# A new instruction order for a retention and WaveMLP kernel: 34 DMA transposes in place of 39, and products of zeros moved ahead

## The chip, the cores and the metric

The kernel runs on one core of one Trainium2 chip. The metric is the device time of one execution in microseconds (us), lower is better; the median over several runs is compared. The core has five engines with instruction queues of their own: TensorE (PE in the profile; its weight loads are PEld), VectorE (DVE), ScalarE (ACT), GpSimd (POOL) and SyncE (SP), which here only issues DMAs. Each queue runs strictly in its own order and waits for others by semaphores.

## The reference

Inputs are q, k, v of shape (4, 8, 768, 64) in float32 (batch, heads, tokens, head width) and four weight matrices. First a linear attention with a decay for each head, then a mixing layer over tokens and channels:

```python
gamma = 1.0 - 2.0 ** (-5.0 - np.arange(H))
for t in range(S):
    state = gamma * state + einsum('bhd,bhe->bhde', k[:, :, t], v[:, :, t])
    y[:, :, t] = einsum('bhd,bhde->bhe', q[:, :, t], state) / np.sqrt(D)
x = y.transpose(0, 2, 1, 3).reshape(B, S, H * D)      # (4, 768, 512)

theta = x @ w_theta
zr, zi = x * cos(theta), x * sin(theta)
u = x + w_tok_r @ zr + w_tok_i @ zi                   # over tokens, in each batch
out = u + maximum(u @ w_ch, 0)
```

The output is (4, 768, 512) in float32.

## The kernel before

The whole program is a list of small functions, and one string, ORDER, says in which order they are called. Since the tile framework is used with its scheduler switched off, a token's place in ORDER is its place in the queues of the engines that it uses: two tokens on the same engine run in the order of the string, two on different engines are tied only by the data and buffers that they share. A token such as `cq.3.p` calls `cq(3, "p")`; the last letter names the engine (p POOL, v DVE, a ACT, s SP).

**Attention.** The work is cut into 24 units: batch, then three blocks of 256 tokens, then two halves of four heads. Unit n is loaded by `Lk`, `Lq` and `Lv` (256 KB each, L156, all on SP's queue), cast or scaled to bf16 by `ck`, `cq` and `cv` (L138, L278, L284), and its k and q are transposed: either on TensorE (`Tk` and `Tq`, four transposes each into one PSUM tile, then one copy `E`), or by one DMA transpose (`Dk`, L308) that SP issues. `G(n)` puts three groups of sixteen small products together: the scores of unit n (at, L322), the output inside the block of unit n-1 (L392) and the state's increment of unit n (L350). `m` masks the scores on DVE (L331), `SU` adds to the state (L362 to L366), `SB` casts the state to a block diagonal bf16 tile sbd (L138 on DVE or POOL, L136 on ACT), `I` multiplies the queries with it (L379), and `XA` copies the result out of PSUM to xT, x transposed (L412).

**Mixing.** For each of 24 blocks C of 128 tokens, `Tx` and `Ex` (TensorE and a copy) or `Dx` (a DMA transpose, L433) turn xT into x; `Hh` makes theta (four products of 512 columns, L440), `CN` takes the sine and cosine on ACT (L447), and `z` multiplies both with x (L454, DVE or POOL). `M(t, s0)` is two products of 512 columns into the output block t for the token block s0 (L487), so block t needs the six z of its batch. `u` adds x (L494), `Tu` and `Eu` or `Du` (a DMA transpose, L509) transpose u, `O` multiplies by w_ch (four products, L514), `f` takes the maximum and adds (L520), and `SO` stores 256 KB from SP's or ACT's queue (L525). The last block is cut into two halves (`Mh`, `uh`, `Tuh`, `Euh`, `Oh`, `fh`, `SOh`), and ends the program.

**Weights.** `Lth` and `Lch` load w_theta and w_ch (1 MB each, `cth` and `cch` cast them in quarters), `Lw` loads 128 rows of w_tok_r or w_tok_i, `cw` casts, `Tw` transposes on TensorE and `Ew` copies out of PSUM.

**Constants and zero products.** `const2` makes the exponents' input (POOL, then one multiplication on DVE), `const3` the two scale tables by two exponentials on ACT, which cq and cv need; `const4` the identity, `const5` the mask, `const1` a tile of zeros and `const6` zeros in sbd. `warm(n)` multiplies the tile of zeros with itself n times into a PSUM tile that nobody reads:

```python
    def warm(n):
        t = psum.tile([P, dm], FT, name="y_ps", tag="y", bufs=1)
        for _ in range(n):
            nc.tensor.matmul(t, K["zero"][:, :P], K["zero"], start=True, stop=True)
```

Buffers tie tokens as well. All transposes through PSUM, and theta of the odd blocks from 7 on, share two PSUM buffers (tag tr), so each waits until the one two before it was copied out; y uses one bank and o another (acc) for most of the program, so `M.t.0` waits for `u` of the block before. kf, qf and vf have nine buffers each, kqT four, uT three.

## Time and profile before

| what | value |
|---|---|
| median of 5 runs | 175.66 us |
| lowest and highest | 174.13 and 177.23 us |
| the profiled execution's own time | 174.13 us |
| its span, first to last instruction | 172.2 us |
| mean granted TensorE clock | 0.970 |
| TensorE, DVE, ACT, POOL busy | 153.1, 116.1, 80.2, 83.3 us |
| DMA transposes: kqT, x_sb, uT | 10, 12, 17 |

The span is 1.9 us shorter than the execution's time; what lies around it doesn't depend on the order. The profile page has the busy time of each engine; slices of the span in which a digit is the busy share in tenths (PEclk is the clock granted to TensorE, in tenths of full speed); the chain of waits, followed back from the last instruction; and groups of instructions with the mean of one in ns and what ended the idle time before them. Matmuls overlap, so the length of one product (379 ns for 512 columns) is more than the 216 ns from one start to the next.

### The profile page before, as it was taken

How to read it: one execution, taken by the hardware profiler on the slowest of the kernel's cores; microseconds unless marked ns; L12 is line 12 of the kernel's file. 1: busy time of each engine (PE TensorE's matmuls, PEld its weight loads, DVE VectorE, ACT ScalarE, POOL GpSimd, SP SyncE). 2: the span in 40 equal slices, each digit the busy share in tenths (PEclk: the TensorE clock that was granted, in tenths of full speed). 3: DMA queues.
4: the chain of work that ended last, by engine and by line, in shares of the span. 5: the costliest groups of instructions: out<-in, count | busy, mean ns of one | idle time of the engine just before them, and what ended most of it. 6: DMA issues, size and time to landing. Idle time of an engine off the chain costs nothing.

```text
span 172.2 us, 4849 instructions
## 1 busy us (share of the span) xinstructions
PE 153.1 (89%) x1996; PEld 87.4 (51%) x1996; DVE 116.1 (67%) x191; ACT 80.2 (47%) x157; POOL 83.3 (48%) x106
## 2 busy tenths in 40 slices
...
PEclk9995769999999999999999999999999999999999
...
GB/s 139 279 290 291 352 328 286 335 365 263 201 245 350 330 207 207 250 289 293 162 274 181 232 163 216 153 317 183 227 177 122 182 108 142 73 232 30 183 162 173
DMA packets 70757, 38.71 MB, mean 225 GB/s; under 512 B 28112, under 2 KB 65232, under 8 KB 70736
## 3 DMA queue, kind: packets, MB, share of 16 engines
...
## 4 chain that ended last, share of the span: by engine, by line
PE 69%; DVE 9%; DMA 8%; SPq 7%; issue 2%; POOLq 1%; ACT 1%; DVEq 0%; ACTq 0%
PE y_ps L487 29%; PE o_ps L514 11%; PE th_ps L440 11%; SPq L156 7%; DMA w<-in_moe_w_theta_dram 5%; PE at_ps L322 4%; DMA x_sb<-xT 3%; PE r_ps L392 3%; DVE sbd L138 2%; PE r_ps L379 2%; PE kq_ps L292 2%; PE y_ps L537 2%; PE r_ps L350 1%; DVE z L454 1%; DVE at L331 1%
## 5 line engine op out<-in xcount | busy, mean ns | idle before, releaser
L487 PE MATMUL y_ps<-z,wtr 128*128 128x512 bf16 x138 | 52.4, 380 | 1.6 <-POOL z L454 1.4
L487 PE MATMUL y_ps<-z,wti 128*128 128x512 bf16 x138 | 52.3, 379 | 0.0
L278 POOL TENSOR_TENSOR kqb<-qf,qsc 128x512 bf16<-128x512 f32 x21 | 22.9, 1091 | 17.6 <-DMA qf<-in_q_dram 17.5
L331 DVE TENSOR_TENSOR at<-at_ps,mask 128x1024 bf16<-128x1024 f32 x24 | 29.2, 1216 | 1.2 <-PE at_ps L322 1.1
L412 ACT CAST xT<-r_ps 128x256 bf16<-128x256 f32 x48 | 17.1, 374 | 27.3 <-PE r_ps L350 15.7
L440 PE MATMUL th_ps<-wth,xT 128*128 128x512 bf16 x96 | 25.4, 397 | 1.2 <-ACT wth L136 1.2
L520 DVE SCALAR_TENSOR_TENSOR ot<-o_ps,u 128x512 f32<-128x512 f32 x23 | 15.8, 687 | 11.8 <-PE o_ps L514 11.3
L494 DVE TENSOR_TENSOR u<-y_ps,x_sb 128x512 bf16<-128x512 f32 x23 | 15.7, 687 | 11.8 <-PE y_ps L487 11.6
L514 PE MATMUL o_ps<-wch,uT 128*128 128x512 bf16 x92 | 23.5, 380 | 0.0
L454 POOL TENSOR_TENSOR z<-cs,x_sb 128x1024 bf16<-128x1024 bf16 x7 | 15.3, 2186 | 15.0 <-DMA x_sb<-xT 8.7
L487 PEld LDWEIGHTS <-wti 128*128 128x128 bf16 x138 | 13.5, 98 | 14.7 <-issue 2.5
L447 ACT ACTIVATE cs<-th_ps,zerob 128x512 bf16<-128x512 f32 x24 | 16.4, 689 | 9.1 <-PE th_ps L440 6.8
L138 POOL CAST kqb<-kf 128x512 bf16<-128x512 f32 x19 | 14.3, 757 | 12.4 <-DMA kf<-in_k_dram 11.7
L487 PEld LDWEIGHTS <-wtr 128*128 128x128 bf16 x138 | 13.5, 98 | 13.0
L284 POOL TENSOR_TENSOR vb<-vf,vsc 128x512 bf16<-128x512 f32 x16 | 17.8, 1120 | 3.5 <-PE y_ps L487 3.0
L447 ACT ACTIVATE cs<-th_ps,halfpi 128x512 bf16<-128x512 f32 x24 | 16.5, 689 | 5.2 <-PE th_ps L440 2.6
L454 DVE TENSOR_TENSOR z<-cs,x_sb 128x1024 bf16<-128x1024 bf16 x17 | 15.3, 907 | 1.5 <-ACT cs L447 1.4
L292 PE MATMUL kq_ps<-ident,kqb 128*128 128x128 bf16 x112 | 11.3, 245 | 5.0 <-DVE kqb L138 4.3
L440 PEld LDWEIGHTS <-xT 128*128 128x128 bf16 x96 | 9.3, 101 | 11.0 <-issue 3.0
L514 PEld LDWEIGHTS <-uT 128*128 128x128 bf16 x92 | 8.5, 98 | 9.7 <-DMA uT<-u 0.3
L322 PE MATMUL at_ps<-kqT 64*64 64x128 bf16 x384 | 10.5, 229 | 3.0 <-ACT kqT L136 1.9
L292 PEld LDWEIGHTS <-kqb 128*128 128x128 bf16 x112 | 8.4, 109 | 8.2 <-DVE kqb L138 4.3
...
## 6 DMA issues: line engine op xcount, KB each, us to landing
...
```

The source lines that it names most:

```text
L138: engines[e].tensor_copy(dst, src)
L278: engines[e].tensor_mul(in_blocks(kqb_of(n)[:, 1]), by_token(raw["qf", n]), _bcast_last(K["qsc"][:, i, :, h * HU:(h + 1) * HU], D))
L284: engines[e].tensor_mul(in_blocks(vb), by_token(raw["vf", n]), _bcast_last(K["vsc"][:, i, :, h * HU:(h + 1) * HU], D))
L292: nc.tensor.transpose(st["kq_ps", n][:, 4 * w + x, :], st["kqb", n][:, w, x * P:(x + 1) * P], K["ident"])
L322: nc.tensor.matmul(at_ps[cols, g, j, a, :], kqT[rows, 0, a, j, cols], kqT[rows, 1, :, j, cols], start=(j == 0 and a == 0), stop=(j == 1 an ...
L331: nc.vector.tensor_mul(at.rearrange("p g j a t -> p (g j) (a t)"), st["at_ps", n].rearrange("p g j a t -> p (g j) (a t)"), _bcast_mid(K["m ...
L412: nc.scalar.copy(st["xT", 2 * i + c][:, 2 * h:2 * h + 2].rearrange("p j (t a) -> p j t a", a=2), st["R", n + 1][:, c, :2 * P].rearrange("p ...
L440: nc.tensor.matmul(th_ps, st["xT", C][:, j, :], K["wth"][:, j, :], start=(j == 0), stop=(j == 3))
L447: nc.scalar.activation(st["cs", C][:, w, :], st["th_ps", C], AF.Sin, bias=K["zerob" if w else "halfpi"], scale=1.0)
L454: engines[e].tensor_mul(st["z", b][:, c], st["cs", C], _bcast_mid(x_of(C), 2))
L487: nc.tensor.matmul(st["y", t], K["wT"][r][:, s0, t0 * P:(t0 + 1) * P], st["z", b][:, s0, r, :], start=(s0 == 0 and r == 0), stop=(s0 == nT ...
L514: nc.tensor.matmul(o_ps, st["uT", t][:, j, :], K["wch"][:, j, :], start=(j == 0), stop=(j == nD - 1))
```

## The change

Only the string ORDER differs. No function is changed, and every needed token is there once; what a token does may be on another engine. Counted from the two strings:

| tokens | before | after |
|---|---|---|
| zero products (calls of warm) | 8 (1) | 44 (8) |
| Dk, Dx, Du | 10, 12, 17 | 11, 9, 14 |
| Tk and Tq, Tx, Tu | 14 and 14, 12, 6 | 13 and 13, 15, 9 |
| SB on ACT, DVE, POOL | 23, 14, 11 | 25, 19, 4 |
| z on DVE, POOL | 17, 7 | 20, 4 |
| cv on DVE, POOL | 8, 16 | 3, 21 |
| Ew on DVE, ACT | 8, 4 | 11, 1 |
| Ex on DVE, ACT | 8, 4 | 6, 9 |
| Eu on DVE, ACT | 3, 3 | 3, 6 |
| SO on SP, ACT | 11, 12 | 14, 9 |

The first eight zero products come ahead of all other work of TensorE, where before the transposes of the first k were ahead of them; the other 36 stand in seven groups up to the first theta products. `const2` moves behind `const4`, `ck.0` and `const5` on POOL. The diff, cut:

```diff
--- before.py
+++ after.py
 ORDER = """
-const2 Lk.0.s const1 Lq.0.s Lv.0.s const3 const6 const4 ck.0.v cv.0.v const5 Tk.0 Lk.1.s Lq.1.s
-cq.1.p warm.8 Lv.1.s Lk.2.s Lq.2.s cq.0.v Lv.2.s cv.1.v Tq.0 ck.1.a E.0.a cq.2.p Lk.3.s G.0 SU.0
-ck.3.p SB.0.0.v ck.2.a Tk.1 Lq.3.s cv.2.p cq.3.p SB.0.1.a Tq.1 I.0 m.0 E.1.a G.1 Tk.2 Lv.3.s
-Lk.4.s Lq.4.s Tq.2 Tk.3 XA.0.1 SU.1 E.2.v m.1 ck.4.v cq.4.p SB.1.0.a SB.1.1.a Lv.4.s XA.0.0 Tq.3
-I.1 G.2 SU.2 SB.2.1.a Lth.s m.2 SB.2.0.p Lw.0.0.s cv.3.p Lk.5.s XA.1.1 XA.1.0 Lq.5.s E.3.v cth.2.a
-Tq.4 cv.4.p Lv.5.s Tk.4 cth.1.p Lw.1.0.s cw.0.0.p ck.5.p cth.0.a I.2 Lk.6.s G.3 Lq.6.s XA.2.1
-cth.3.v cq.5.p Lw.0.1.s m.3 SU.3 Tx.0 Hh.1 E.4.a Lv.6.s cv.5.p SB.3.0.v cw.1.0.p Hh.0 Tx.1 Ex.0.a
-XA.2.0 SB.3.1.v I.3 Lk.7.s G.4 Ex.1.v ck.6.p Tq.5 CN.0.1 CN.0.0 XA.3.1 Tk.5 m.4 E.5.a cq.6.p SU.4
-Lq.7.s Tw.0.0 cw.0.1.p cv.6.p SB.4.1.a SB.4.0.v Tw.1.0 Ew.0.0.v XA.3.0 CN.1.1 Ew.1.0.v Tk.6 I.4
-z.0.v ck.7.p G.5 Tq.6 SU.5 SB.5.1.p cq.7.p CN.1.0 Lw.1.1.s Lv.7.s E.6.v m.5 Lk.8.s Hh.3 SB.5.0.a
-Tx.3 Hh.2 XA.4.0 Tx.2 Ex.3.v CN.3.1 Lq.8.s z.1.p Ex.2.v Lw.0.2.s Lw.1.2.s XA.4.1 Lw.0.3.s ck.8.p
-CN.3.0 I.5 G.6 Tq.7 cw.1.1.a cq.8.p XA.5.1 Tk.7 E.7.a Tw.1.1 Tx.5 XA.5.0 CN.2.1 m.6 CN.2.0 Lv.8.s
-z.3.v Ew.1.1.v SU.6 cw.0.2.p Hh.5 Tx.4 Ex.5.v cv.7.v Lw.1.3.s SB.6.0.a Tk.8 Lk.9.s Lq.9.s Hh.4
-Ex.4.v SB.6.1.a CN.5.0 CN.5.1 Tq.8 z.2.v Lv.9.s I.6 G.7 Tw.0.2 M.0.0 Lk.10.s CN.4.1 CN.4.0 Lq.10.s
-E.8.v z.5.p Lw.0.4.s Tw.0.1 M.0.1 cw.1.2.p cv.8.p SU.7 ck.9.p M.0.2 cq.9.p M.0.3 SB.7.1.v cw.0.3.a
-XA.6.1 Ew.0.2.v z.4.v SB.7.0.v Lv.10.s Tw.0.3 XA.6.0 m.7 Ew.0.1.a M.0.4 ck.10.p Ew.0.3.a M.0.5 u.0
...
-Lch.s M.1.2 M.1.3 SB.8.1.v Tu.0 Lq.11.s Ew.1.3.a M.1.4 XA.7.1 cv.9.p M.1.5 ck.11.p cch.0.p Lv.11.s
...
-CN.6.1 Ex.7.a CN.6.0 M.3.0 Tk.11 cch.1.a m.10 Du.1 SU.10 M.3.1 M.3.2 Ew.0.4.v SB.10.0.v M.3.3
-Lq.13.s Lv.13.s Tq.11 XA.9.1 E.11.v XA.9.0 ck.12.p M.3.4 M.3.5 z.7.p ck.13.p Tx.6 cw.1.4.a
-SB.10.1.a Tw.1.4 I.10 cch.2.a u.3 G.11 Ew.1.4.a O.0 Ex.6.v XA.10.0 Lk.14.s cq.13.p SU.11 Tw.0.5
-Lq.14.s M.4.0 Ew.0.5.v Tx.9 M.4.1 Dx.8 m.11 XA.10.1 M.4.2 M.4.3 Lv.14.s Lk.15.s Dk.13 Tq.12 M.4.4
-SB.11.1.a Ex.9.a Tk.12 cw.1.5.a Hh.9 cv.12.v E.12.a M.4.5 SB.11.0.v Lq.15.s f.0 Lv.15.s CN.9.0
-I.11 CN.9.1 Tw.1.5 G.12 u.4 O.1 XA.11.0 Ew.1.5.v M.5.0 SU.12 M.5.1 z.6.p Tu.2 XA.11.1 f.1 cq.14.p
...
-m.23 M.13.3 Dx.20 XA.22.0 M.13.4 SO.11.s CN.21.0 O.16 CN.21.1 SO.9.s Dx.21 SB.23.1.p SB.23.0.p
-I.23 G.24 M.13.5 XA.23.1 f.16 XA.23.0 Dx.22 O.12 M.22.0 f.12 Du.15 z.20.v u.13 Dx.23 Hh.23 z.21.p
-Hh.22 CN.23.0 M.20.0 M.22.1 CN.22.0 M.18.0 M.20.1 M.18.1 M.18.2 CN.22.1 CN.23.1 M.22.2 M.18.3
-M.22.3 O.14 z.22.v SO.10.s M.18.4 M.22.4 z.23.p M.20.2 M.22.5 M.18.5 Du.13 f.14 u.18 u.22 O.15
-M.20.3 SO.16.a Du.18 SO.14.a M.17.0 M.17.1 M.19.0 f.15 SO.12.s M.19.1 O.13 Du.22 M.17.2 M.17.3
-f.13 M.17.4 M.17.5 M.19.2 SO.13.a u.17 M.20.4 M.19.3 O.18 f.18 M.21.0 M.19.4 M.19.5 M.21.1 O.22
-M.21.2 u.19 M.21.3 SO.15.s M.21.4 M.21.5 Du.17 f.22 O.17 Du.19 u.21 M.20.5 f.17 u.20 O.19 Mh.0.0
-Mh.1.0 Mh.0.1 f.19 SO.22.a Mh.0.2 Mh.0.3 SO.18.a Mh.0.4 Du.21 Du.20 Mh.1.1 Mh.1.2 Mh.1.3 Mh.0.5
-uh.0 SO.19.a Mh.1.4 Mh.1.5 O.21 O.20 Tuh.0 uh.1 SO.17.a f.21 SO.21.s Tuh.1 Euh.0 f.20 Euh.1 Oh.0
-SO.20.a Oh.1 fh.0 fh.1 SOh.1 SOh.0
+const4 Lk.0.s ck.0.p const1 const5 Lq.0.s Lv.0.s const6 const2 Lk.1.s const3 warm.8 cq.0.v cv.0.p
+Tk.0 Lq.1.s ck.1.p Lv.1.s Lk.2.s cv.1.p Lq.2.s cq.1.v warm.6 Tq.0 E.0.a warm.5 Tk.1 G.0 cq.2.p
+Tq.1 ck.2.v SU.0 E.1.a Lw.0.0.s SB.0.0.a Lv.2.s Lk.3.s ck.3.p warm.9 Tq.2 Lq.3.s cq.3.p SB.0.1.a
+m.0 Lv.3.s I.0 cv.2.v Lk.4.s G.1 Lq.4.s SU.1 SB.1.1.p ck.4.p Lth.s Tk.2 m.1 XA.0.0 XA.0.1 Lw.1.0.s
+warm.9 Tq.3 E.2.v cv.3.v Tk.3 SB.1.0.a cq.4.p E.3.a I.1 G.2 SU.2 XA.1.0 Lv.4.s SB.2.1.p SB.2.0.p
+Lk.5.s cth.0.p Lq.5.s cth.3.p cw.1.0.p cv.4.p Tk.4 XA.1.1 warm.3 Tx.0 m.2 Tq.4 E.4.v Lv.5.s warm.1
+I.2 cw.0.0.a cth.2.v Ex.0.a cth.1.a G.3 SU.3 Lw.0.1.s Lk.6.s ck.5.p XA.2.1 cq.5.p cv.5.p Lq.6.s
+Tw.0.0 Lv.6.s Lw.1.1.s XA.2.0 SB.3.1.a cw.0.1.p warm.3 Hh.0 Tw.1.0 Lk.7.s SB.3.0.v CN.0.0 m.3
+CN.0.1 Ew.1.0.v Lq.7.s Hh.1 cq.6.p Ew.0.0.v I.3 G.4 Tk.5 Lv.7.s Lk.8.s Tq.5 CN.1.1 z.0.v Lw.0.2.s
+SU.4 CN.1.0 XA.3.1 E.5.a m.4 Tx.1 Hh.3 cv.6.p Ex.1.v SB.4.1.v Lq.8.s SB.4.0.a Lw.1.2.s XA.3.0
+Lw.0.3.s Tw.0.1 ck.6.a Tx.3 CN.3.1 z.1.v CN.3.0 I.4 Ex.3.v G.5 Lv.8.s Ew.0.1.v SU.5 Hh.2 m.5
+cw.1.1.p ck.7.p XA.4.0 cq.7.p Tq.6 Tk.6 Lw.1.3.s cv.7.p ck.8.p cw.0.2.p SB.5.0.v cq.8.p Lk.9.s
+XA.4.1 SB.5.1.a Lq.9.s Tx.2 E.6.v Lv.9.s I.5 z.3.v Ex.2.a G.6 CN.2.0 Tw.1.1 Tq.7 Lw.0.4.s CN.2.1
+Tk.7 Lch.s XA.5.1 Lk.10.s m.6 XA.5.0 Hh.5 Ew.1.1.v Lq.10.s SU.6 E.7.a SB.6.0.a Tx.5 cw.1.2.p
+CN.5.1 CN.5.0 SB.6.1.v Hh.4 I.6 Tw.0.2 Ex.5.v z.2.v CN.4.1 z.5.p CN.4.0 Lw.1.4.s cv.8.p Ew.0.2.v
+G.7 cq.9.p Lv.10.s Tx.4 SU.7 M.0.0 ck.9.p cv.9.p Ex.4.v cch.2.p cw.0.3.v Tk.8 z.4.v Tq.8 Lk.11.s
+M.0.1 Lq.11.s ck.10.p XA.6.0 E.8.a SB.7.1.v SB.7.0.a cq.10.p M.0.2 XA.6.1 cq.11.p m.7 Tw.0.3
+Lv.11.s M.0.3 M.0.4 M.0.5 u.0 Tw.1.2 Lw.0.5.s I.7 cw.1.3.v G.8 M.1.0 M.1.1 M.1.2 M.1.3 SU.8
+Ew.1.2.v M.1.4 Ew.0.3.a Lk.12.s Tu.0 XA.7.0 Tq.9 m.8 M.1.5 SB.8.1.v Eu.0.v Hh.6 Tk.9 SB.8.0.v
+cw.0.4.a Tw.1.3 Lq.12.s u.1 XA.7.1 ck.11.p M.2.0 CN.6.0 E.9.v M.2.1 I.8 Ew.1.3.v ck.12.p cch.1.a
+cq.12.p G.9 cv.11.p cch.3.v cch.0.v Lw.1.5.s Dk.11 CN.6.1 Lv.12.s SU.9 M.2.2 Hh.7 cw.1.5.p m.9
+CN.7.1 Tx.6 Ex.6.v M.2.3 M.2.4 SB.9.0.v SB.9.1.v M.2.5 cv.12.p Dk.12 u.2 O.0 XA.8.0 Lk.13.s CN.7.0
+f.0 Tk.10 M.3.0 XA.8.1 Tq.10 I.9 ck.13.p Tw.0.4 Lq.13.s cw.1.4.v E.10.a cv.10.v M.3.1 M.3.2 M.3.3
+Tw.1.4 Ew.0.4.v G.10 Lv.13.s Tu.1 Eu.1.a Lk.14.s M.3.4 Ew.1.4.v M.3.5 m.10 Tx.7 u.3 XA.9.1 O.1
+XA.9.0 Tx.8 M.4.0 SU.10 M.4.1 SB.10.0.a Ex.7.v M.4.2 Ex.8.a Lq.14.s cq.13.p ck.14.p SB.10.1.v
+M.4.3 cw.0.5.a Lv.14.s Tu.2 M.4.4 Dk.13 Eu.2.a cv.13.p z.7.v Tw.0.5 f.1 cq.14.p I.10 Tx.9 G.11
+Ex.9.a z.6.v cv.14.p Hh.8 Ew.0.5.v Tw.1.5 SU.11 m.11 M.4.5 Hh.9 XA.10.0 SB.11.1.a Ew.1.5.v XA.10.1
+SB.11.0.a I.11 CN.8.1 u.4 G.12 CN.9.0 XA.11.1 M.5.0 Lk.15.s Lq.15.s CN.8.0 CN.9.1 SU.12 Lv.15.s
+M.5.1 Dk.14 Tx.11 Lk.16.s M.5.2 cq.15.p M.5.3 Ex.11.a Lq.16.s z.8.v z.9.v Tu.3 O.2 SB.12.1.v f.2
+Eu.3.a cq.16.p SB.12.0.a M.5.4 XA.11.0 SO.0.a Lv.16.s M.5.5 Hh.11 Tx.10 I.12 m.12 Hh.10 Lk.17.s
+CN.11.1 CN.11.0 G.13 cv.15.p Lq.17.s u.5 Lv.17.s CN.10.1 Lk.18.s M.6.0 Ex.10.a CN.10.0 z.11.v
...
+CN.16.0 cq.22.p Hh.17 CN.16.1 u.11 SU.19 Dk.21 CN.17.0 M.12.0 M.12.1 CN.17.1 cv.21.p SB.19.0.a
+XA.18.1 m.19 M.12.2 Du.11 SO.6.a Lv.22.s Lk.23.s z.16.v O.9 z.17.v SB.19.1.v M.12.3 f.9 XA.18.0
...
+SB.23.0.a M.13.0 XA.22.0 z.18.v SO.10.a CN.21.0 M.13.1 M.13.2 Dx.20 I.23 SO.11.a Du.14 G.24
+XA.23.0 XA.23.1 f.16 M.20.0 M.20.1 O.12 f.12 M.13.3 Dx.22 z.20.v M.13.4 Hh.23 CN.21.1 z.21.p
+M.13.5 Hh.22 Dx.23 M.22.0 CN.22.0 CN.22.1 M.22.1 CN.23.0 u.13 Du.15 M.18.0 M.18.1 M.18.2 CN.23.1
+M.22.2 O.14 M.18.3 M.22.3 z.22.p M.20.2 f.14 z.23.v M.18.4 O.15 SO.12.s Du.13 M.18.5 M.22.4 u.18
+M.22.5 M.20.3 M.17.0 M.17.1 u.22 M.17.2 M.17.3 M.17.4 M.17.5 SO.16.s f.15 u.17 O.13 M.19.0 f.13
+M.19.1 Du.18 M.21.0 O.18 SO.15.a M.19.2 SO.14.a M.19.3 M.21.1 M.20.4 M.19.4 Du.22 M.21.2 f.18
+M.19.5 SO.18.a M.21.3 O.22 u.19 Du.17 Du.19 SO.13.s f.22 SO.22.s M.21.4 M.21.5 M.20.5 u.21 const7
+O.17 Mh.0.0 Du.21 f.17 Mh.0.1 Mh.0.2 O.19 u.20 f.19 Mh.1.0 Mh.0.3 Mh.0.4 Mh.0.5 Mh.1.1 Tu.20
+Mh.1.2 uh.0 Eu.20.a SO.19.s Mh.1.3 Mh.1.4 SO.17.a Tuh.0 Mh.1.5 O.20 uh.1 Tuh.1 Euh.0 Euh.1 f.20
+O.21 SO.20.a Oh.0 f.21 SO.21.s Oh.1 fh.0 fh.1 SOh.1 SOh.0
 """.split()
 
```

## The prediction

> **What bounds the kernel now.** I read the page's busy rows and its slices first, then busy time by stage, then single stretches of the timeline, then the landing times of the loads.
>
> ```profile
> PE 153.1 (89%) x1996; PEld 87.4 (51%) x1996; DVE 116.1 (67%) x191; ACT 80.2 (47%) x157; POOL 83.3 (48%) x106
> ...
> PEclk9995769999999999999999999999999999999999
> ```
>
> TensorE is busy for 89% of the span, but the granted clock is low in slices 4 to 6 (13 to 26 us), and busy time there is not work done. By stage (columns: length, then each engine's busy us with its instruction count, clock, DMA share, GB/s):
>
> ```profile
> 0.00:26.50 26.50, 16.67 (x252) 10.68 (x252) 13.70 (x29) 12.36 (x23) 15.33 (x37) 0.81 0.95 278
> 26.50:45.00 18.50, 16.21 (x326) 11.36 (x324) 17.78 (x30) 15.81 (x30) 17.72 (x18) 1.00 1.06 316
> 45.00:60.00 15.00, 14.97 (x245) 9.32 (x245) 11.10 (x21) 10.41 (x20) 9.48 (x12) 1.00 1.03 277
> 60.00:70.00 10.00, 8.29 (x151) 5.11 (x149) 7.62 (x10) 5.77 (x10) 7.89 (x7) 1.00 1.28 219
> 70.00:144.00 74.00, 74.00 (x910) 39.15 (x908) 54.21 (x85) 35.18 (x74) 30.74 (x35) 1.00 0.99 208
> 144.00:148.00 4.00, 2.64 (x13) 1.16 (x12) 0.69 (x1) 0.00 (x0) 2.12 (x1) 1.00 0.42 79
> ...
> 165.20:172.20 7.00, 3.13 (x22) 1.68 (x19) 2.73 (x6) 0.65 (x2) 0.00 (x0) 1.00 0.42 153
> ```
>
> Four places lose TensorE time: the start (fed by loads, clock low), 26.5 to 45 us (DVE 17.8 of 18.5 and POOL 17.7 are the full ones), 60 to 70 us, and 144 to 148 us with the tail. From 70 to 144 us it is busy for all 74.00 us: a shorter time can only come from less loss in the four places or from less work.
>
> To price work I take start-to-start times at full clock from the timeline: two y products 0.43 us, four theta or channel products 0.86, four transposes 0.22, a G (48 small products) 0.70, an I 0.23, six weight transposes 0.34. Summed over the order, the kernel before has 139.3 us of needed TensorE work and eight zero products; all else of 172.2 is loss. The same prices in the new order let one place be compared with another: G.8 has 22.0 us of needed work ahead of it in both orders, G.13 has 51.8 before and 52.1 after.
>
> **1. The start, up to G.8.** Single stretches (start us, length us, what):
>
> ```profile
> 4.75 3.62 PE L257 MATMUL y_ps<-zero 128*128 128x512 bf16 x8
> ...
> 9.90 0.42 PE L322 MATMUL at_ps<-kqT 64*64 64x128 bf16 x16 [1.10 <-ACT kqT L136]
> ...
> 12.70 0.64 PE L322 MATMUL at_ps<-kqT 64*64 64x128 bf16 x16 [0.75 <-ACT kqT L136]
> ...
> 22.90 3.35 PE L440 MATMUL th_ps<-wth,xT 128*128 128x512 bf16 x8 [1.22 <-ACT wth L136]
> ```
>
> Eight zero products take 3.62 us, 0.43 each, the half rate; right after them the sixteen at products take 0.42 us, and from 12.7 us, when TensorE had waited a lot, 0.64. So products of zeros do raise the clock, and waiting loses it. The first theta products (two tokens, 3.35 us) run at half rate; at full rate they are 2 x 0.86 = 1.73, so 1.6 us to be had. A rule speaks against making much of this: the Trainium skill (TensorE: Matmul & The Clock Gate, "What's actually happening") says that the clock is granted by free-running windows of about 3.4 us and that the ramp costs under 1% of a typical span. The rows agree on its size here, since 1.6 us is 0.9% of 172.2; by that page's figure alone the gain would be at most 1.7 us, by the row 1.6.
>
> What the new order adds there: 8 + 6 + 5 zero products before G.0, then 9, 9, 3, 1 and 3 in later waits, 44 in all. At 0.22 us the 36 extra ones are 7.8 us, at 0.43 they are 15.4. Their cover is what TensorE loses before 22.9 us: 22.9 minus the 5.5 us of needed work ahead of the theta products. The end of that stretch is set by w_theta, which lands at 21.7 after 15 loads of 256 KB; in the new order 14 such loads and one of 384 KB are ahead of it, the same within 0.2 us.
>
> One step makes the start later. const2 (the exponents' input) moves on POOL behind ck.0, which waits for the first k load (lands 3.84) and casts for 0.61; then const5 takes 1.5 and const2 0.55. Behind const2 wait DVE's multiplication, ACT's table load and two exponentials (1.94 us together), and for those cq.0 and cv.0: cq.0 starts at 8.45 in place of 7.06, and G.0 at about 10.9 in place of 9.90. Walking on with loads every 0.85 us and the durations of the rows: G.1 13.8 (12.70 before), G.2 17.2 (16.86), G.3 19.8 (20.59), Hh.0 22.2 to 23.4, G.4 25.5 (26.62). The delay is swallowed by waits for loads, and the clock gives about 1.1 us.
>
> From there DVE sets the pace. From z.0 to m.7, whose output G.8 waits behind, the new order has 26 DVE instructions of 15.8 us in all; each starts 0.08 us before its predecessor ends, so 13.7 us, from 25.9. Before, the like stretch (30.10 to 44.98) has 11.3 us by that count and took 14.9: 3.6 us went to waits, mostly these:
>
> ```profile
> 39.34 2.13 POOL L454 TENSOR_TENSOR z<-cs,x_sb 128x1024 bf16<-128x1024 bf16 x1 [0.58 <-DVE z L454]
> ...
> 42.20 1.57 POOL L284 TENSOR_TENSOR vb<-vf,vsc 128x512 bf16<-128x512 f32 x1
> ```
> ```profile
> 40.55 1.00 DVE L138 CAST sbd<-s 64x128 bf16<-64x128 f32 x1
> ...
> 42.78 1.06 DVE L138 CAST sbd<-s 64x128 bf16<-64x128 f32 x1
> ```
>
> A 64x128 cast takes 0.21 us alone and 1.00 here: it ends when POOL's instruction ends. This counts against the new order: casts of sbd on DVE go from 14 to 19, z products on DVE from 17 to 20, while POOL stays nearly as loaded. Ten instructions between SBUF tiles stand in this stretch after, eight before; those eight took 2.8 us more than they take alone, 0.35 each. The Trainium skill (SBUF — State Buffer, "Who interferes with whom") goes further: whichever of the two engines issues first holds the shared ports for its whole instruction, so by that page each of the ten may wait out a POOL instruction, an estimate of up to 10 us with the 1.04 us of a scaled q. With the same 3.6 us G.8 starts at 43.3, with half a us more at 43.8 (45.03 before). Bounds: 42.5 with no such wait, 45.9 with 0.45 us on each and the clock's gain lost. I take **-1.2 us** (-2.5 to +0.9), nearest to the measured 3.6.
>
> **2. G.8 to G.13.** Before, 45.03 to 77.42 for 29.8 us of work: 2.6 us lost, of which this cast is one large piece:
>
> ```profile
> 65.49 2.57 POOL L454 TENSOR_TENSOR z<-cs,x_sb 128x1024 bf16<-128x1024 bf16 x1
> ...
> 66.01 2.20 DVE L138 CAST sbd<-s 64x256 bf16<-64x256 f32 x1
> ...
> 68.27 0.40 PE L379 MATMUL r_ps<-kqT,sbd 128*128 128x128 bf16 x4 [1.10 <-DVE sbd L138]
> ```
>
> z.6 and z.7 move from POOL to DVE (2.12 us there, 0.69 here), so this collision goes. But DVE gets 17.6 us up to G.12 by the count above beside 23.4 of TensorE work, and eleven locked instructions; at the 0.35 us each of above, 3.9. That is 92% full. I take 1.2 us lost, so **-1.4** (from -2.6 with nothing lost to +1.3 with all 3.9). SP waits here for POOL's casts before the first two transposes (Dk.11 and Dk.12, about 54 to 57 us), and the loads of units 12 to 14 queue behind them. Unit 13 then lands by about 63 us and is needed at 72, so I cost that at nothing; without that slack it would be up to the 3 us of the wait.
>
> **3. Work.** Three Tx, three Tu, one Tk and one Tq fewer: (3 + 3 - 2) x 0.22 = **+0.9 us** on the bound engine, in stretches with no gap to take it. The five DMA transposes saved are worth nothing by themselves, since from 70 to 144 us TensorE waits for none; their price (1.2 us of SP each) is hidden.
>
> **4. The wait at 144 to 148.** M.22.5 waits 1.36 us for z.23, which POOL makes in 2.1 us after x lands (the chain of waits: start, length, what):
>
> ```profile
> 139.68 5.47 DMA x_sb<-xT
> 145.26 2.15 POOLq L604
> 147.46 1.02 PE y_ps L487 x4
> ```
>
> After, z.23 is on DVE (0.69) and first used 10.4 us of work behind G.24 (9.1 before), and Dx.23 no longer stands behind Du.15 on SP. With the same 5.5 us of flight it would land 8.5 us behind G.24, f.14 and z.23 end at about 10.1. I take **-0.9** (-1.5 to 0).
>
> **5. Tail.** Before, the last y product is followed by O.21, O.20, the last transposes, a 0.56 us gap, and Oh. After, the transposes and their copies lie beside O.20 and O.21, so Oh follows directly: **-0.7** (-0.9 to 0). The rest of 70 to 144 us: 0, at worst +1 (z.17 now has 3.0 us from its theta products to its use, 4.1 before, and needs 2.9).
>
> **Sum.** -1.2 - 1.4 + 0.9 - 0.9 - 0.7 = -3.3 from the profiled execution's 174.13 (span 172.2): 170.8. That execution is the lowest of five; the median 175.66 is 1.5 higher, so I forecast a median of **172.4**, 1.9% faster. About 1% is what a measurement here can tell from no change.
>
> **Rivals.** (a) DVE becomes the bound from 26 to 70 us: parts 1 and 2 at +0.9 and 0, the rest as above, +0.2: 175.9. For it: 17.78 of 18.5 busy. Against: three POOL z products fewer. Chance 0.21. (b) **Slower**: the zero products run at half rate through the waits. It decides if the clock is not up by G.1: the two groups of nine then cost 2 x 9 x 0.21 = 3.9 us more than counted, beyond the cover because w_theta's landing is passed, and the 1.6 us are not won. -3.3 + 1.1 + 3.9 = +1.7 by these alone, some 177.4. For it: the clock fell at 12.7 after such a start. Against: zero products did raise it, and the new groups fill those waits. Chance 0.13, and 0.04 for stalls that I don't see. (c) The new order does not keep TensorE any fuller: the order of a queue is not its time, and a search prices by its own figures. Parts 1, 2 at zero and 4, 5 at half: 0 + 0.9 - 0.8 = +0.1, 175.8; it shares (a)'s chance. Forecast: 0.62, at 1% or more. So faster 0.62, same 0.21, slower 0.17. The range takes the favourable bounds of parts 1, 2, 4 and 5 together (-6.6, at 169.1) and reaches beyond (a) nearly to (b): 169.0 to 177.0.
>
> **What would show it.** Full clock from about 10 us on, and the first eight theta products in some 1.7 us in all; G.8 near 43.8; no DVE cast over 2 us; no wait for z.23; Oh without a gap. Wrong if G.3 starts after 22 us, or DVE fills 60 to 75 us.

## The result, and the profile after

| | before | after |
|---|---|---|
| median, lowest, highest (94 and 52 executions) | 176.96, 173.32, 180.27 us | 174.96, 172.98, 181.43 us |
| ratio after to before, 95% interval | | 0.9992 [0.9969, 1.0015] |
| the profiled execution's own time, span | 174.13, 172.2 us | 173.48, 171.8 us |

By the ratio this is no change; the forecast said 1.9% faster. The ratio takes only executions within 1.5% of their kernel's fastest, which keeps 21 of the 94 of before and 40 of the 52 of after (their medians are 174.67 and 174.68): the best executions of the two are equal, the ordinary one is 2.0 us better after. Two later comparisons of the same pair, with fewer executions, gave 0.989 [0.9834, 0.9946] and 0.9936 [0.9867, 1.0005]. So the change is worth between nothing and about 1%.

The page of after, its busy row and its row of granted clock:

```profile
PE 158.5 (92%) x2048; PEld 88.9 (52%) x2048; DVE 118.9 (69%) x197; ACT 78.2 (45%) x159; POOL 79.1 (46%) x103
...
PEclk9969999999999999999999999999999999999999
```

TensorE is busy 5.4 us longer in a span that is 0.4 us shorter: what was idle time at the start is now zero products, and the low clock is left in one slice in place of three. By stage (columns as in the prediction: length, PE, PEld, DVE, ACT, POOL busy with counts, clock, DMA share, GB/s):

```profile
0.00:26.50 26.50, 22.61 (x344) 12.91 (x344) 16.30 (x29) 11.75 (x22) 17.21 (x42) 0.94 1.01 285
26.50:45.00 18.50, 15.11 (x286) 10.02 (x275) 17.52 (x28) 14.81 (x29) 16.74 (x17) 1.00 1.09 336
45.00:60.00 15.00, 14.40 (x218) 8.85 (x221) 14.03 (x27) 5.97 (x11) 9.23 (x11) 1.00 1.02 264
60.00:70.00 10.00, 10.00 (x192) 6.41 (x184) 8.61 (x15) 6.79 (x14) 5.77 (x7) 1.00 1.11 262
70.00:144.00 74.00, 72.22 (x928) 38.15 (x919) 50.07 (x81) 37.21 (x81) 29.33 (x29) 1.00 0.87 188
144.00:148.00 4.00, 4.00 (x20) 1.86 (x19) 1.29 (x2) 0.00 (x0) 0.79 (x1) 1.00 0.50 159
```

The waits at 60 to 70 and at 144 to 148 us are gone, as forecast. From 26.5 to 45 us TensorE is emptier than before (15.11 against 16.21) beside a VectorE that is still full, and the stretch that was full, 70 to 144 us, now misses 1.78 us.

The start, on TensorE's timeline (start, length, instruction):

```profile
13.08 2.11 PE L258 MATMUL y_ps<-zero 128*128 128x512 bf16 x9
...
16.39 2.11 PE L258 MATMUL y_ps<-zero 128*128 128x512 bf16 x9
...
23.53 1.03 PE L441 MATMUL th_ps<-wth,xT 128*128 128x512 bf16 x4
...
24.73 1.03 PE L441 MATMUL th_ps<-wth,xT 128*128 128x512 bf16 x4
```

Nine zero products take 2.11 us, the full rate, and the first eight theta products 0.86 + 0.86 us from start to start, as forecast (3.35 before). But both groups of nine stand on the chain of waits, and so do five more at 9.88 us: 6.9 us of zero products lie on it in all up to 23.7 us. What a thing on that chain costs is another question, which e2 and e8 below answer.

The new hole, on ScalarE's timeline (the bracket is the idle time before the row and what ended it):

```profile
73.24 0.36 ACT L413 CAST xT<-r_ps 128x256 bf16<-128x256 f32 x1
76.49 0.38 ACTq L526 DMA_DIRECT2D out_dram<-ot  x1
76.97 0.69 ACT L448 ACTIVATE cs<-th_ps,zerob 128x512 bf16<-128x512 f32 x1 [3.37 <-DMA kf<-in_k_dram]
```

The first store, SO.0, is issued from ScalarE's queue. Its data were ready long before, yet it left at 76.49 us, 0.02 us after the load of k of unit 17 (issued by SP at 71.40) had landed at 76.47: the trace shows the two transfers with the same semaphore. Behind it in ScalarE's queue waited sines, a copy of uT and with them three steps of TensorE (1.0 us of waits at 78 to 82 us; from start to start of G.13 and G.14 it is 1.5 us, 6.53 against 5.04 in e1 below). The hole is not the same in every execution: in the two later traces of the same kernel these two starts are 5.85 and 5.66 us apart.

Milestones of TensorE (us from the span's start; the difference of the differences is what each stage gained or lost):

| first product of | before | after | difference | forecast |
|---|---|---|---|---|
| G.3 | 20.59 | 21.84 | +1.25 | -0.8 |
| first theta | 22.90 | 23.53 | +0.63 | -0.7 to +0.5 |
| G.4 | 26.62 | 25.91 | -0.71 | -1.1 |
| G.8 | 45.03 | 45.60 | +0.57 | -1.2 |
| G.13 | 77.42 | 76.24 | -1.18 | -2.3 |
| Oh | 167.85 | 167.14 | -0.71 | -3.3 |
| end of the span | 172.22 | 171.76 | -0.46 | -3.3 |

### The profile page after: what moved, and what is told of

It is laid out like the page before. It is cut to its first block, busy times and chain, and to the rows that moved or that the text cites. A ratio compares the mean times of both kernels' runs of the same rounds, so it can differ in the third digit from the quotient of the medians.

```text
span 171.8 us, 4952 instructions
## 1 busy us (share of the span) xinstructions
PE 158.5 (92%) x2048; PEld 88.9 (52%) x2048; DVE 118.9 (69%) x197; ACT 78.2 (45%) x159; POOL 79.1 (46%) x103
## 4 chain that ended last, share of the span: by engine, by line
PE 69%; DVE 9%; DMA 7%; ACT 4%; POOL 3%; issue 3%; SPq 2%; DVEq 0%; ACTq 0%; POOLq 0%
PE y_ps L488 29%; PE o_ps L515 10%; PE th_ps L441 8%; DMA kf<-in_k_dram 5%; PE y_ps L258 4%; PE at_ps L323 4%; PE kq_ps L293 3%; DMA x_sb<-xT 3%; DVE z L455 2%; PE r_ps L393 2%; DVE at L332 2%; ACT cs L448 2%; PE r_ps L380 2%; PE w_ps L472 2%; PE y_ps L538 2%
## 5 line engine op out<-in xcount | busy, mean ns | idle before, releaser
L279 POOL TENSOR_TENSOR kqb<-qf,qsc 128x512 bf16<-128x512 f32 x22 | 23.9, 1084 | 27.5 <-DMA qf<-in_q_dram 26.3
L441 PE MATMUL th_ps<-wth,xT 128*128 128x512 bf16 x96 | 24.7, 379 | 1.0 <-ACT cs L448 0.8
L285 POOL TENSOR_TENSOR vb<-vf,vsc 128x512 bf16<-128x512 f32 x21 | 22.9, 1092 | 5.6 <-DMA vf<-in_v_dram 3.3
L455 DVE TENSOR_TENSOR z<-cs,x_sb 128x1024 bf16<-128x1024 bf16 x20 | 17.3, 879 | 5.2 <-ACT cs L448 3.5
L139 POOL CAST kqb<-kf 128x512 bf16<-128x512 f32 x20 | 13.7, 687 | 13.1 <-DMA kf<-in_k_dram 11.1
L258 PE MATMUL y_ps<-zero 128*128 128x512 bf16 x44 | 13.8, 459 | 1.3 <-DVE zero L194 1.3
L441 PEld LDWEIGHTS <-xT 128*128 128x128 bf16 x96 | 8.8, 98 | 10.2 <-issue 0.9
L455 POOL TENSOR_TENSOR z<-cs,x_sb 128x1024 bf16<-128x1024 bf16 x4 | 8.5, 2122 | 9.0 <-DMA x_sb<-xT 5.1
L293 PE MATMUL kq_ps<-ident,kqb 128*128 128x128 bf16 x104 | 9.8, 230 | 2.5 <-DVE kqb L279 2.5
L365 DVE TENSOR_TENSOR s<-r_ps,s 128x128 f32<-128x128 f32 x16 | 4.6, 286 | 10.8 <-ACT xT L413 5.8
```

The costliest lines, as they stand in the source:

```text
L279: engines[e].tensor_mul(in_blocks(kqb_of(n)[:, 1]), by_token(raw["qf", n]), _bcast_last(K["qsc"][:, i, :, h * HU:(h + 1) * HU], D))
L285: engines[e].tensor_mul(in_blocks(vb), by_token(raw["vf", n]), _bcast_last(K["vsc"][:, i, :, h * HU:(h + 1) * HU], D))
L441: nc.tensor.matmul(th_ps, st["xT", C][:, j, :], K["wth"][:, j, :], start=(j == 0), stop=(j == 3))
L455: engines[e].tensor_mul(st["z", b][:, c], st["cs", C], _bcast_mid(x_of(C), 2))
```

## The experiments

Each row is one kernel beside the kernel before on the same chip; five groups of runs, each on a chip of its own. "No change" is only to be judged against the rows of the changed kernel itself (174.59 and 175.42).

| kernel | chip | median us | before there | ratio, 95% interval |
|---|---|---|---|---|
| e1 store SO.0 on SP | A | 173.0 | 176.62 | 0.9791 [0.9737, 0.9846] |
| e2 without the 36 products | A | 177.25 | 176.62 | 0.9899 [0.9831, 0.9966] |
| e3 u.13 ahead of z.20 | A | 173.3 | 176.62 | 0.9817 [0.9765, 0.987] |
| e4 z.5 on DVE | A | 174.9 | 176.62 | 0.993 [0.9894, 0.9966] |
| e5 the changed kernel | B | 174.59 | 176.86 | 0.989 [0.9834, 0.9946] |
| e6 before with 36 products | B | 185.93 | 176.86 | 1.0502 [1.0428, 1.0575] |
| e7 e1 and e3 together | B | 172.57 | 176.86 | 0.9776 [0.9722, 0.983] |
| e8 e7 with 29 zero products | B | 172.24 | 176.86 | 0.9769 [0.9725, 0.9812] |
| e9 2.4 us more on DVE | C | 178.33 | 177.83 | 1.0214 [1.0019, 1.0408] |
| e10 2.6 us more on TensorE | C | 176.78 (two runs) | 177.83 | none |
| e11 39 DMA transposes, in place | C | 184.48 | 177.83 | 1.0581 [1.0463, 1.0698] |
| e12 e8 and three DVE steps moved | C | 172.78 | 177.83 | 0.9871 [0.9761, 0.9982] |
| e13 the changed kernel | D | 175.42 | 177.0 | 0.9936 [0.9867, 1.0005] |
| e14 39 DMA transposes, two earlier | D | 177.5 | 177.0 | 1.0035 [0.9971, 1.0099] |
| e15 e8 again | D | 173.28 | 177.0 | 0.9824 [0.9736, 0.9913] |
| e16 e8 and two DVE steps moved | D | 171.31 | 177.0 | 0.9749 [0.9664, 0.9833] |
| e17 e6 with three casts on ACT | E | 180.83 | 176.86 | 1.0284 [1.0209, 1.0359] |
| e18 e16 with two casts on ACT | E | 172.6 | 176.86 | 0.98 [0.9748, 0.9851] |

**The store in ScalarE's queue (e1).** One letter:

```diff
- XA.11.0 SO.0.a Lv.16.s M.5.5
+ XA.11.0 SO.0.s Lv.16.s M.5.5
```

> The changed order with one letter changed: the store of output block 0 (SO.0) is issued from SP's queue instead of ACT's. In the changed kernel's trace ACT stands still from 73.6 to 76.5 us ahead of that store, until the load of k of unit 17 has landed, and TensorE then loses 1.6 us between G.13 and G.14. Theory (this store holds ACT's queue, and with it the copies and sines that TensorE waits for): ACT's gap ahead of 77 us goes, G.14 starts 1.3 to 1.6 us earlier beside G.13, and the time falls by 0.6 to 0.9% against the changed kernel, to a ratio of 0.990 to 0.994 to the kernel before. Rival (the cover is thin, another wait comes up in its place within the next units, or the store now holds SP and its loads): G.14 gains but G.24 does not, ratio 0.997 to 1.002.

On SP's queue the same store leaves at once, and the sine at the same place starts 1.8 us earlier, waiting only for its theta (SP's timeline, then ScalarE's):

```profile
69.80 0.44 SPq L525 DMA_DIRECT2D out_dram<-ot  x1
```
```profile
75.18 0.69 ACT L447 ACTIVATE cs<-th_ps,zerob 128x512 bf16<-128x512 f32 x1 [1.55 <-PE th_ps L440]
```

TensorE has no wait left at 76 to 84 us, and from there to the end every milestone is 1.4 us earlier than in after's trace (the last f 166.97 against 168.34; span 170.4 against 171.8). The ratio, 0.979, is better than the theory's 0.990 to 0.994, more than the trace accounts for. This run had no copy of the changed kernel beside it; e7 and e8 below did.

**u.13 ahead of z.20 (e3), and both edits (e5, e7).** In after, z.20 (1.80 us on DVE, beside z.21 on POOL) stands ahead of u.13, and TensorE waits 0.77 us for u.13 at 142.5 us. e3 swaps the two on DVE.

> The changed order with u of block 13 ahead of z of block 20 on DVE (it was behind it). In the changed kernel z.20 takes 1.80 us there, because POOL's z.21 runs from 139.18 to 141.29, and u.13 and with it the first product of block 18 wait behind it: TensorE loses 0.94 us at 141.6. Theory (that queue place is the loss, and it is on the path to the end): the wait before M.18.0 goes to under 0.1 us and the time falls by 0.5%, ratio 0.993 to 0.996. Rival (the products behind it then wait for z.20 or z.23 instead): TensorE loses 0.5 us or more at 142 to 146 us, ratio 0.997 to 1.001.

> The changed kernel unaltered, beside the variants that follow and the kernel before, on one chip. Theory: the change is worth 0 to 1.5 us, so the ratio to the kernel before is 0.990 to 1.000; the store put on SP's queue, which was measured at 0.979, is then worth 1 to 2%. Rival: on this chip the changed kernel is itself at 0.975 to 0.985, and then neither the store nor the order of u.13 has been shown to be worth anything beyond what the single traces show (1.4 us and nothing at the end).

> The changed kernel with both edits that were tried singly: SO.0 issued by SP instead of ScalarE, and u.13 ahead of z.20 on VectorE. Theory (two separate stalls of TensorE, 1.4 us at 77 to 83 us and 0.9 us at 142 us, of which the first alone reaches the end, as each single trace showed): 1.2 to 1.8 us under the changed kernel, M.18 without a wait, end at 170.2 to 170.6 us. Rival (both reach the end): 2.2 to 2.6 us under it. Other rival (the timed gains of the single edits, 1.8 to 2.1% against before, were the chip's and not the edits'): within 0.5 us of the changed kernel.

In e3's trace u.13 starts 1.36 us earlier (140.40), but TensorE now waits 0.6 us for z.20, f.14 is no earlier (145.46 against 145.28), and the span is 171.9: the rival, the wait only changes its name. Its ratio, 0.9817, is better than both theory and rival had it, and nothing in the trace says why; it had no copy of the changed kernel beside it either. e7, with both edits, is 2.0 us under the changed kernel on the same chip. Its theory allowed 1.2 to 1.8, its rival 2.2 to 2.6; what the store alone explains by the trace is 1.4. Whether u.13 adds anything is not settled; no trace shows it.

**The zero products (e2, e6, e17, e8, e15).** e2 drops all but the first eight from the changed kernel; e6 puts the 36 into the order of before, at the same kinds of step; e17 is e6 with three casts taken off DVE; e8 thins them in e7 to 29.

```diff
e2  - warm.6, warm.5, warm.9, warm.9, warm.3, warm.1, warm.3
e6  + warm.6 Tq.0 ... warm.5 Tk.1 ... warm.9 Tk.2 ... warm.9 Tq.3 ... warm.3 Tq.4 ... warm.1 I.2 ... warm.3 Hh.1
e17 e6 and  - cth.3.v SB.3.0.v SB.3.1.v   + cth.3.a SB.3.0.a SB.3.1.a
e8  e7 and  - warm.6 warm.5 warm.9 warm.9  + warm.3 warm.3 warm.4 warm.4
```

> The changed order without the 36 later products of zeros; the first eight stay. Theory of the prediction (they keep the clock up and lie in waits): the clock falls to half in the first 26 us, G.4 comes later than 26.6, the time grows by 1 to 1.6 us, ratio 1.005 to 1.009. Rival (they buy the clock but pay for it with their own time: 6.9 us of them stand on the chain of waits, G.1 and G.2 come 2.8 and 2.1 us later than in the kernel before, and DVE sets G.8 in any case): G.1 and G.2 come earlier by 1 to 2 us, the first theta products take 3.3 us instead of 1.9, G.8 stays within 0.5 us of 45.6, ratio 0.996 to 1.002.

> The order of before with 36 more zero products ahead of the same kinds of step (6 at the first transpose of q, 5 at the second of k, 9 at the third, 9 at the fourth of q, 3, 1 and 3 up to the first theta products), nothing else of the change. Theory (the products raise the clock and stand in the chain themselves, one against the other): full clock from about 12.5 us, the first eight theta products in about 1.75 us instead of 3.35, but G.1 to G.3 are 1 to 2 us later than in before, and G.8 starts at 44.3 to 45.7 us (before 45.0); ratio 0.990 to 1.000. Rival (the products fit in the waits, and what made G.1 to G.3 late is the new order of loads and casts): G.1 to G.3 within 0.5 us of before, G.8 at 42.5 to 43.5 us, ratio 0.980 to 0.987.

> The kernel with both edits and with 29 zero products instead of 44 (8, 3, 3, 4, 4, 3, 1, 3 instead of 8, 6, 5, 9, 9, 3, 1, 3). Theory (the zero products stand on the chain at 13 to 23 us, and the clock would be full with fewer): full clock from 12.5 us still, G.1, G.2 and G.3 1 to 2.5 us earlier, G.8 0.5 to 2 us earlier. Rival (what ends the waits there is loads and casts, the zero products run beside them): G.1 to G.3 within 0.4 us and the time within 0.3 us of the kernel with 44. Second rival (the fewer products no longer hold the clock): a stretch of half clock in 12 to 26 us and a time 0.5 to 2 us above.

> The order of before with the 36 more zero products, and three VectorE casts at 23 to 28 us (theta's fourth block and both state casts of unit 3) on ScalarE. Theory (the 9.3 us cast beside GpSimd's unbroken row was the loss; the products alone raise the clock and stand in the chain, one against the other): 9 to 12 us under the 185.9 us of the kernel with the products alone, that is 174 to 177 us and a ratio of 0.985 to 1.000; first eight theta products in under 2 us without a wait between. Rival (the products themselves push the start back): above 180 us. Other rival (ScalarE, given 1.4 us more ahead of the first sines, becomes the wait): 177 to 180 us.

e2: without the products the clock is at 0.5 in slices 3 to 5 and again in 7, and the executions spread from 172.87 to 178.9 us. That says the products do hold the clock; the spread lets no more be said about the time. Neither its theory nor its rival held for the starts of the first units (us; "walked" is the prediction's walk):

| first product of | before | walked | after | e1 | e8 | e2 |
|---|---|---|---|---|---|---|
| G.0 | 9.90 | 10.9 | 12.38 | 11.48 | 11.71 | 11.68 |
| G.1 | 12.70 | 13.8 | 15.45 | 14.56 | 15.38 | 15.01 |
| G.2 | 16.86 | 17.2 | 18.98 | 18.09 | 18.70 | 18.75 |
| G.3 | 20.59 | 19.8 | 21.84 | 20.95 | 21.56 | 22.39 |

With all 36 products gone G.1 and G.2 come only 0.4 and 0.2 us earlier, not the 1 to 2 of the rival, and G.3 comes 0.5 us later: the same steps now run at half rate. So in this order the 6.9 us on the chain are not what the products cost. The start of after is late at G.0 already, and it has two causes there. The five products ahead of it ran at half rate, and the transposes behind them need a cast of k that POOL ends at 11.14. In e1, the same order up to here, the clock was full by then, and all four starts are 0.9 us earlier (after's row, then two of e1's):

```profile
9.68 2.34 PE L258 MATMUL y_ps<-zero 128*128 128x512 bf16 x5
```
```profile
9.47 1.24 PE L257 MATMUL y_ps<-zero 128*128 128x512 bf16 x5
11.15 0.40 PE L292 MATMUL kq_ps<-ident,kqb 128*128 128x128 bf16 x4 [0.44 <-POOL kqb L138]
```

What is left of the lateness in e1, 0.6 us at G.0, comes with that cast, since TensorE waits for it.

e6 was 9 us slower than before, and neither theory had it. G.2's state update came 3.8 us later than in before (21.95 against 18.19), which is the products on the chain, and then this (DVE's timeline, then POOL's up to the same moment):

```profile
24.21 9.31 DVE L137 CAST wth<-w 128x512 bf16<-128x512 f32 x1
```
```profile
31.65 1.04 POOL L283 TENSOR_TENSOR vb<-vf,vsc 128x512 bf16<-128x512 f32 x1
32.63 0.61 POOL L137 CAST kqb<-kf 128x512 bf16<-128x512 f32 x1
```

A cast that takes 0.43 us in before took 9.31. POOL ran one instruction after another from 22.31 to 33.24 us without a gap, and the cast ended 0.28 us after the last of them. Later starts on TensorE had moved the cast into POOL's row. e17 takes that cast and the next two off DVE: 5 of the 9 us come back, the theta products run in one piece (8 in 1.90 us), and what is left is 2.2 us at G.2's state update (20.42 against 18.19) and 2.6 at unit 8's (48.90 against 46.26). So on the order of before the 36 products cost more than the clock returns (G.1 to G.3 come 1.2, 2.7 and 2.2 us later than in before); "they fit in the waits" falls, and "one against the other" was too kind: at 180.83 us e17 misses its theory (174 to 177) and meets its first rival (above 180).

e8 shows the other side. With 15 products fewer G.1 to G.3 come 0.1 to 0.3 us earlier than in after where its theory had 1 to 2.5, the state updates of units 3 and 6 come 0.3 and 0.5 us earlier, those of units 8 and 10 not at all (46.59 against 46.53, 62.15 against 62.20), and the time is 0.3 us under e7: its rival. e15 repeats e8 beside the changed kernel on another chip:

> The changed kernel unaltered, as the mark for the three kernels beside it. Theory: 0.985 to 1.000 of before, as in the earlier two comparisons (0.9992 and 0.989). Rival: below 0.985 on this chip, which would make the chips differ by more than the change is worth.

> The kernel with the store on SP, u.13 ahead of z.20 and 29 zero products, once more. Theory: 1.5 to 2.5 us under the changed kernel beside it (2.35 us before, 172.24 against 174.59). Rival: within 0.8 us of it, and the earlier distance was the chance of a few executions.

It is 2.1 us under it there, 2.35 on chip B: the gain of store, u.13 and fewer products together is repeated; of its parts only the store's is explained by a trace.

**Who sets the pace from 27 to 46 us (e9, e10).** e9 does the mask product of units 5 and 6 twice, the second into a tile that nobody reads; e10 adds six zero products behind each of the two instead.

```diff
e9      def m(n): ...
+           if n in (5, 6): nc.vector.tensor_mul(at2, at_ps of unit n, mask)
e10 - m.5 cw.1.1.p ... m.6 XA.5.0
    + m.5 warm.6 cw.1.1.p ... m.6 warm.6 XA.5.0
```

> The changed kernel with the mask product of units 5 and 6 done twice (the second copy goes to a tile that nothing reads): 2.4 us more on VectorE at 34 to 38 us (2 x 1.2, the row of the mask product), nothing else. Theory (VectorE is what TensorE runs after from 26.5 to 45 us, 17.5 busy of 18.5): state update of unit 8 starts 1.8 to 2.4 us later than the 46.5 to 46.9 us of the changed kernel. Rival (TensorE's own chain, started late by the zero products, sets it): 0 to 0.8 us later.

> The changed kernel with 6 more zero products behind the mask products of units 5 and of 6 (at 34 and 37 us), 12 x 0.216 = 2.6 us more on TensorE, nothing else. Theory (VectorE sets the pace there): the state update of unit 8 starts 0 to 0.9 us later than the 46.5 to 46.9 us of the changed kernel. Rival (TensorE's chain sets it): 1.8 to 2.6 us later. If this kernel and the one with the padded VectorE are both late by over 1.8 us, the two engines take turns in one chain and neither is the bound alone.

The state update of unit 8 on DVE, in after, in e9 and in e10:

```profile
46.53 0.28 DVE L365 TENSOR_TENSOR s<-r_ps,s 128x128 f32<-128x128 f32 x1
```
```profile
51.37 0.27 DVE L370 TENSOR_TENSOR s<-r_ps,s 128x128 f32<-128x128 f32 x1
```
```profile
46.62 0.28 DVE L364 TENSOR_TENSOR s<-r_ps,s 128x128 f32<-128x128 f32 x1
```

The starts differ, so the fair measure is the time since unit 4's state update: 18.2 us in after (from 28.31), 21.1 in e9 (from 30.27), so the 2.4 us on DVE cost 2.9. e10 started at 27.16, like e1, which reaches unit 8 at 46.07 without the products: 2.6 us on TensorE cost 0.55. These are one trace each, but far apart: VectorE is the bound there. e1 says the same from the other end: an early start of 1.15 us at unit 4 is 0.46 at unit 8 and nothing at unit 10 (62.23 against 62.20). VectorE has no idle time there in e1 either; the lead goes into steps that run longer beside POOL, such as z.1 (1.42 us against 1.20 in after).

**Relief for VectorE (e4, e12, e16, e18).** e4 takes z.5 off POOL, where it ran beside three locked DVE steps. e12 moves theta's third block to POOL, a token cast (1.00 us at 40.86) to ScalarE, and z.4 behind the mask product of unit 7; e16 is the latter two; e18 adds two casts on ScalarE.

```diff
e4  - z.5.p                           + z.5.v
e16 - cw.0.3.v Tk.8 z.4.v ... m.7     + cw.0.3.a Tk.8 ... m.7 z.4.v
e12 e16 and - cth.2.v                 + cth.2.p
e18 e16 and - cth.2.v SB.3.0.v        + cth.2.a SB.3.0.a
```

> The changed order with z of block 5 on DVE (0.69 us) instead of POOL (2.12 us). In the changed kernel z.4, a cast of a weight row and a cast of sbd take 1.53, 1.00 and 0.95 us on DVE at 40.9 to 44.3, against 0.69, 0.55 and 0.21 alone, and G.8 waits behind them. Theory (POOL's long product holds DVE off): although DVE gets one instruction more, these three fall together by 1 us or more, G.8 starts at 44.6 to 45.0 instead of 45.6 and the time falls by 0.3 to 0.6%, ratio 0.993 to 0.997. Rival (the scaled v and q that follow on POOL hold DVE off just as long, or the time gained at G.8 is lost by G.13): G.8 at 45.4 or later, or ratio 0.998 to 1.002.

> The kernel with the store on SP, u.13 first and 29 zero products (measured at 0.977 of before, 172.2 us), and three steps of VectorE moved away from GpSimd's: the cast of the third block of theta's weights to GpSimd itself, one cast of token weights (1.0 us at 41 us) to ScalarE, and z.4 (1.5 us) behind the mask product of unit 7. Theory (from 27 to 46 us VectorE sets the pace, and what stands ahead of the mask product of unit 7 is on the chain): the state update of unit 8 starts at 44.4 to 45.4 us instead of 46.6, and of it 0.5 to 1.5 us reach the end: 170.7 to 171.7 us, ratio 0.968 to 0.974. The theta products start within 0.5 us of 23 us in every execution. Rival (the next stretch, 45 to 60 us, has VectorE at 14.0 of 15.0 and takes it back): unit 8 early, unit 10 not, time 172.0 to 172.6. Other rival (TensorE is held by something else there): unit 8 within 0.3 us of 46.6.

> The same kernel with the token-weight cast of 41 us on ScalarE and z.4 behind the mask product of unit 7, nothing else. Theory (what stands ahead of that mask product on VectorE is on the chain to G.8, but the work behind it is the same): G.8's first product at 43.5 to 44.5 us instead of 45.6, and 0 to 0.4 us of it at the end, because VectorE is at 14.0 of 15.0 in the next stretch. Rival (the 1 us lead lasts, TensorE being full from 46 us on): 0.8 to 1.5 us under the kernel beside it. Other rival (z.4 is now late for its token mixing): later than the kernel beside it by 0.3 us or more.

> The best version so far (store on SP, u.13 first, 29 zero products, one token cast on ScalarE, z.4 behind the mask product of unit 7) with the third block of theta's weights and one state cast of unit 3 on ScalarE too. Theory (no VectorE cast is left beside GpSimd's row at 22 to 28 us; ScalarE has 1 us more ahead of the first sines): no VectorE instruction over 2 us before 30 us, the time within 0.6 us of the kernel without the edit, 171 to 172 us, ratio 0.968 to 0.978. Rival (ScalarE's 1 us moves the first sines and all behind them): 172.5 to 173.5 us.

e4 shows no gain: it stands where the changed kernel stood on its two chips (0.993 against 0.989 and 0.9936); in its trace G.8 follows G.4 by 19.6 us, after 19.7. Both come late there (G.8 at 49.83), because a cast on DVE had taken 5.42 us at 22 us. That is no trait of e4. The third run of the changed kernel itself, e13, has it too:

```profile
22.27 4.64 DVE L139 CAST wth<-w 128x512 bf16<-128x512 f32 x1
```

The same cast takes 0.60 us in after and 0.42 in e5. In e13 G.4 then starts at 30.32 (25.91 in after), and that execution took 178.10 us, where those of after and e5 took 173.48 and 174.57. So the loss that e6 shows is a risk of the changed order too, and after's trace escaped it. How often it happens can't be said from single profiles. In e12's trace the lock was only handed on, to the next cast in the row (DVE's, then POOL's timeline):

```profile
23.32 4.83 DVE L138 CAST sbd<-s 64x256 bf16<-64x256 f32 x1
```
```profile
27.18 0.82 POOL L138 CAST wrow<-wtok 128x768 bf16<-128x768 f32 x1
28.64 1.04 POOL L278 TENSOR_TENSOR kqb<-qf,qsc 128x512 bf16<-128x512 f32 x1 [0.64 <-DMA qf<-in_q_dram]
```

It ended 0.15 us after the last instruction ahead of POOL's first pause, which POOL owed to a late q load. That execution, 175.15 us, is the longest of e12's six, so its trace doesn't test what e12 expected at unit 8; the median, 172.78, is above the theory's 170.7 to 171.7. In e16 the mask product of unit 7 runs 2.7 us earlier than in after, and G.8 starts at 45.55 all the same (expected at 43.5 to 44.5): ahead of it TensorE waits 1.28 us at 44.15 for z.4, which the products of block 0 need. Both z.4 and the mask product stand ahead of G.8, and putting one first only hands the wait to the other. The medians (171.31 beside 173.28 for e15) are better than that trace accounts for, which at 173.39 us is the longest of e16's six; their intervals overlap, and e18, which adds to e16, stands at 172.6 on another chip, above its theory (171 to 172) and in its rival's range: not settled. e18 has no DVE step over 2 us before 30 us, as expected.

**39 DMA transposes again (e11, e14).** Five transposes go back to SP's queue, with their copies dropped; e14 also issues two of them earlier.

```diff
e11 - Tu.6 Eu.6 Tu.8 Eu.8 Tx.10 Ex.10 Tx.13 Ex.13 Tx.14 Ex.14   + Du.6 Du.8 Dx.10 Dx.13 Dx.14
e14 e11 and Du.6 behind Dx.12, Dx.14 behind Du.9
```

> The changed kernel with five transposes put back on the DMA queue (u of units 6 and 8, x of units 10, 13 and 14), without their products on TensorE (5 x 4 of 0.055 us = 1.1 us) and their evictions (2 on ScalarE or VectorE each 0.4 to 0.6 us). Theory (from 70 to 144 us TensorE is full and its work is the time; the DMA transposes wait for nobody): 0.6 to 1.1 us under the changed kernel, which was at 174.6 beside a before of 176.9, so a ratio of 0.983 to 0.986. Rival (the transposes on the queue land 4 to 5 us after they are issued and hold SP while they wait, so what TensorE saves is given back): the same as the changed kernel, 0.988 to 0.993. Other rival: later by 0.5 us or more, 0.993 to 1.000.

> The changed kernel with the same five transposes on the DMA queue, two of them issued earlier: u of unit 6 behind x of unit 12 (about 90 us instead of 102), x of unit 14 behind u of unit 9 (about 107 us instead of 117). Theory (the transposes land before their readers; TensorE has 1.1 us less to do where it is full, and loses nothing else): 0.5 to 1.1 us under the changed kernel beside it. Rival (a transpose on the queue costs SP's time and its landing of 4 to 5 us shows up at other steps): 0.5 to 3 us above it. If within 0.4 us: the five are worth nothing either way, and the change from 39 to 34 neither.

TensorE's waits in e11 and in e14 (us in total, times, longest):

```profile
PE y_ps L486 <- DVE u L493: 5.0, 1, 5.0
PE o_ps L513 <- DMA uT<-u: 4.5, 1, 4.5
```
```profile
PE r_ps L378 <- ACT xT L411: 2.7, 1, 2.7
PE y_ps L486 <- DVE u L493: 1.8, 1, 1.8
```

A transpose on the queue takes SP 1.2 us and lands 3 us after; put where the one on TensorE stood, 0.2 us of work there, it is late. The wait of 5.0 in e11 is for x of block 14, issued at 117.18 and landed at 120.43. Issued earlier (e14) most of this goes, and the kernel is still 2.1 us above the changed kernel beside it. But the longest wait of e14, 2.7 us, is for no transpose. It is SO.0's case again with another store, which left ScalarE's queue 0.02 us after a load of k had landed at 118.80 (the two have one semaphore), and held a copy that TensorE needed:

```profile
118.82 0.37 ACTq L524 DMA_DIRECT2D out_dram<-ot  x1
119.23 0.37 ACT L411 CAST xT<-r_ps 128x256 bf16<-128x256 f32 x1 [4.70 <-DMA kf<-in_k_dram]
```

In after the same store waits for the same load too, but ScalarE stands only 1.1 us and TensorE not at all. In e14 SP issues that load at 115.78, behind two more transposes, where after has it at 112.24, while G.19 is 1.3 us earlier in e14 (109.89 against 111.15). So SP's time for the transposes is not hidden, as its rival had it. SO.0's own hole is absent in both kernels (it leaves at 72.87 and 73.64 us). Of the 1.1 us of TensorE's work that is saved, 0.6 is seen from G.14 to G.19 (27.76 us against 28.38 in after); what it is worth in an order made for it was not tried.

**A version that beats both.** e8 is under the changed kernel by 2.3 us and 2.1 us on two chips and at 0.977 and 0.982 of before; e16 and e18, built on it, at 0.975 and 0.980.

## Why the prediction was wrong

The trace's sum was forecast at -3.3 us and is -0.46. By its parts:

- **Part 1, -1.2 forecast, +0.57 measured: the step that failed is the walk through the start and, above all, the time of VectorE's stretch from G.4 to G.8.** G.0 came at 12.38 (walked 10.9), which put G.1 to G.3 1.7 to 2.0 us behind the walk. I had the clock full from 10 us; it was so in e1, but in after only from 12.4, which is 0.9 us, and POOL's cast of the second k, for which TensorE waits, took 1.07 us where it takes 0.61 alone. "The delay is swallowed by waits for loads" came true late, between G.3 and G.4: there only 0.4 of it is left (25.91, walked 25.5). The other 1.4 us are VectorE's: z.0 at 27.07 (25.9), behind a table load of 1.28 us on ScalarE that I had not walked (0.8 more behind G.4 than walked), and 18.5 us from z.0 to G.8 (17.9). e9 and e10 show that this stretch is VectorE's, and in e1 a lead of 1.15 us ahead of it is gone by unit 10. So the 1.1 us that I let the clock give ahead of it could not reach the end whole: rival (a) was right up to 46 us.
- **Part 2, -1.4 forecast and +0.3 of part 3's work, so -1.1; measured -1.75: right in what happens, short in size.** Of the 30.6 us 0.5 was lost, where I took 1.2. The cast of 2.20 us is gone, z.6 and z.7 on DVE, and 60 to 70 us is full. Here rival (a) was wrong: DVE is at 8.61 of 10.
- **Parts 3 to 5 and the stretch from 70 to 144 us, forecast together -1.0 behind G.13, measured +0.47 up to Oh.** The step that failed is "the rest of 70 to 144 us: 0, at worst +1 (z.17)". I looked for lateness among the tokens that moved and costed queue changes for SP alone; SO.0 in ScalarE's queue held it 3.4 us. e1 removes it and gets 1.4 us back: with it the sum is -0.9 against the -1.0 of the forecast. Part by part it agrees less well. Oh follows the last products without a gap, as part 5 said; that its start moved by 0.71, the size that part 5 had, is chance, since this is the sum of all parts. From the start of the last y product to Oh it is 1.95 us after and 2.78 before. z.23's wait of 1.36 is gone as part 4 said, but a wait of 0.77 for u.13, which no part had, came ahead of it.
- **"The five DMA transposes saved are worth nothing by themselves"** is not refuted, but e11 and e14 show what I did not say: at a place chosen for TensorE they cost far more than nothing (e11, 1.058 of before), and at a better one still 2 us (e14), in part because "their price (1.2 us of SP each) is hidden" fails there.
- **Signs.** No DVE cast over 2 us was the sign that held by chance: it holds in after's trace, not in e13's (4.64 us). Full clock from 10 us and G.8 near 43.8 did not come in after, and G.3 at 21.84 was just short of the sign against (22); no wait for z.23, Oh without a gap and DVE not full from 60 us (8.61 of 10) did.
- **Rival (b)** is out: the products ran at the full rate from 12.4 us. On the order of before they cost time at that rate too (e6, e17), which I had only allowed at half rate; on the new order their cost to G.1 to G.3, net of what the clock returns, is at most 0.4 us (e2, e8).
- **The median.** I took 175.66 minus the gain; over 94 executions before's median was 176.96, so 1.3 us of the forecast's level came from five executions. That the median of after, 174.96, lies within the range says little: before's own, 176.96, does too.
